# A new order for the first list of a fused attention, channel-mix and expert kernel, with one sigmoid tile moved to another ring

## The chip, the core and the metric

The kernel runs on one core of a Trainium2 chip. The metric is the device time of one execution in microseconds (us). Five engines work side by side, each in the order of its own instruction stream: TensorE (PE in the profile, with its weight loads as PEld), VectorE (DVE), ScalarE (ACT), GpSimd (POOL) and SyncE (SP, which issues most of the DMAs here).

## What is computed

Three layers follow one another. Attention inside chunks of 64 positions, a channel-mix layer, and four attention experts of which each token uses two. Cut to what matters:

```python
# 1: attention in chunks of 64
scores = scale * q_c @ k_c^T ; attn = softmax(scores) ; x = attn @ v_c        # B=8, H=8, S=576, D=64
# 2: channel mix, 512 -> 1024 -> 512
x_prev = x shifted by one position
xk = mu_k * x + (1 - mu_k) * x_prev ;  xr = mu_r * x + (1 - mu_r) * x_prev
k = relu(xk @ w_k) ;  v = (k * k) @ w_v ;  r = sigmoid(xr @ w_r)
x2 = r * v
# 3: four experts, two of them per token
for e in range(4): out += gate_e * (softmax(causal(x2 wq_e (x2 wk_e)^T)) @ (x2 wv_e) @ wo_e)
```

The change touches how layers 1 and 2 start. The channel-mix weights arrive as 64-bit floats and are turned into pairs of 32-bit numbers (high and low part) on the chip; every product of the mix is three TensorE products (high by high, high by low, low by high).

## The kernel before

Layers 1 and 2 work on 4608 tokens. A tile is 128 tokens (36 of them), a pair is two tiles, a unit is 384 tokens or three tiles (12 units). The order in which the first three units are worked on is written out by hand in the list `START` (L21): each word is a step, a letter with numbers, and `follow` (L492) calls the function of each step in turn. `in_line` (L482) ties each instruction to the one before it on the same engine, so every engine, SP with its DMA issues among them, runs its instructions exactly in the order of the list. Then `follow(TWO_UNITS, ...)` (L511) runs a second list four times for two units each, with unit numbers 2, 4, 6, 8 added and tile numbers 12, 18, 24, 30. The chain of `in_line` goes on from `START` into it.

The steps:

- `L`i, `A`i, `G`i, `B`i, `H`i, `O`i: one of 20 weight chunks of 128 x 512 (0 to 3 are w_r, 4 to 11 w_k, of which 8 to 11 hold columns 512 to 1023, 12 to 19 w_v). `L` issues its DMA of 512 KB on SP (L417), `A` is one ACT instruction (L423), `G` two DVE instructions (L427, L428), `B` one DVE (L432), `H` one POOL (L84), `O` one DVE (L443). Chunks 0 to 3 land in tiles of their own; chunks 4 to 19 share two staging tiles (`stb=2`), each free again after `B`.
- `lq`t, `lk`t, `lv`t: the loads of tile t of q, k and v on SP, two staging tiles each (`ldb=2`, `vb=2`). For t below 12 a tile is one to four DMAs (L158, L174). From t = 12 on, q and k are loaded by eight DMAs of 32 KB each (L151) and v by one or two (L166).
- `Tq`, `Tk`, `Eq`, `Ek`: the transposes of q and k on TensorE (L187) and their copies on ACT (L192); from t = 12 on `Tq` and `Tk` are one DVE transpose each (L197) and there is no `E` step. `S`j, `X`j, `U`j, `E`j, `Z`j, `Y`j: scores of pair j on TensorE and its softmax on DVE and ACT. `Tp`, `Ep`: the transposes of the result. `V`j: its product with v on TensorE (L270), the last reader of the two v tiles of pair j. `W`j: the result into `XT` (ACT, L82).
- `prev`u, then `a`, `b`, `c`, `d` with k or r, unit and block g: the mix with the shifted tokens (ACT L304, DVE L308, ACT L315, DVE L319).
- `r`u,m and `s`u,m: 12 TensorE products and the sigmoid (ACT, L344). `k`u,m, `K`u,m, `J`u,m: 12 products, three ACT instructions (L361 to L363), one DVE (L367). `v`u,m,h: 12 products, half h of w_v's rows. `y`, `z`, `x`, `D`: the product with the sigmoid (DVE L384), its split (POOL, DVE L393) and the store (POOL, L398).

The products of r, k and v go through three banks of PSUM (`mix`, `bufs=3`); a bank is free after `s`, the first instruction of `K`, or `y`. The sigmoids of a unit stand in one tile `sig`, of which there is one buffer, from the unit's first `s` to its last `y`. The ring `XT` has four buffers (`xb=4`), each for one unit's attention result.

The second list begins, with its tile numbers read as 13, 12 and so on and its unit numbers as 2 and 3 the first time:

```python
Tq1 Tq0 lq2 Tk1 k0,0 Tk0 prev1 ar1,3 ak1,0 k0,1 br1,3 K0,0 bk1,0 lk2 cr1,3 k0,2 J0,0 K0,1 ...
```

In the list before, the order on SP is `... L19 lk13 lq13 lv10 lv11 lv13 lv12`, with `lq12` and `lk12` earlier, and pair 5's `V5` stands between `v1,0,0` and `v1,0,1`.

Of the kernel before, what the change touches and what calls it, by code (L numbers as in the profile page):

```python
# [8 lines left out]
F32 = mybir.dt.float32  # L9
# [51 lines left out]
CFG = dict(ps=(2, 3, 1, 2), P=5, sm=3, load=5, lag=(3, 4), out=(5, 1), qk1=(1, 1), qk0=(9, 1.1), v=(10, 0.9), order=((3, 0), (2, 0), (0, 0), (4, 0), (1, 0), (3, 1), (2, 1), (0, 1), (1, 1)), after=1, conv='v', clo='v', chi='g', x2hi='g', x2lo='v', ylo='g', yhi='v', xt='aa', r2='av', klo='vv', amul='vv', nearly=2, x2b=1, yb=4, qb=4, direct=((0, 1), (1, 1), (1, 1)), tailAV=4, kp=2, yt=1, yf=2, zb=1, om=(3, 2, 1, 0, 4), hp=1000, x2d=2, early=(2, 1), dact=3, rate0=0.43, rate=0.45, sh=(10, 12, 2), sh2=(11, 1, -1), pro='cccqqaacavvcaaaaacaacaaaascc', alag=2, seq=0, end=2, outL=(11, 2), outE=2, kcp='aa', dsc='v', ldb=2, vb=2, cn=512, stb=2, xb=4, pa=5, tb=2, first_j=7, dve_j=6)  # L61
# [38 lines left out]
def attn_mix(tc, at, x2T, q, k, v, mu_k, mu_r, w_k, w_v, w_r, ident, attended_all, mixed_k):  # L100
# [5 lines left out]
    KD = DM // 128  # L106
# [8 lines left out]
    with ExitStack() as ctx:  # L115
        wts = ctx.enter_context(tc.tile_pool(name="wts", bufs=1))
        mx = ctx.enter_context(tc.tile_pool(name="mx", bufs=1))
# [5 lines left out]
        wkr = wkr_open.enter_context(tc.tile_pool(name="wkr", bufs=1, side="right"))  # L123
# [4 lines left out]
        mu = wkr.tile([128, 2, KD], F32, name="mu")  # L128
# [49 lines left out]
        qT, kT, PP, PT, XT = {}, {}, {}, {}, {}  # L178
# [147 lines left out]
        sig, kk = {}, {}  # L326
# [53 lines left out]
        X2 = {}  # L380
# [80 lines left out]
        def from_T(d, nm):  # L461
# [579 lines left out]
```

## Time and profile before

| | before |
|---|---|
| time, median of three runs | 991.43 us (989.77 to 992.68) |
| the profiled execution | 991.2 us, of which the span from first to last instruction is 987.9 us |
| busy over the span | PE 941.6 us (95%), DVE 668.1 (68%), ACT 625.8 (63%), POOL 190.8 (19%) |
| chain that ended last | PE 83% of the span, DVE 9%, DMA 4%, ACT 2% |
| mean granted TensorE clock | 0.991 of full speed |

The page cuts the span into 40 slices of 24.7 us; the digit of a slice is the busy share of an engine in tenths. Times in the rows below count from the start of the span. A row of a timeline says when an instruction began, how long it took, its engine, line and tiles, how many instructions are merged in it, and in brackets how long the engine was idle before it and which work ended the wait.

### The profile page before, as it was taken

What the parts mean: (1) busy time and instruction counts of PE and PEld (TensorE: products, weight loads), DVE (VectorE), ACT (ScalarE), POOL (GpSimd) and SP (SyncE); (2) the same over time, 40 slices, a digit from 0 to 9 for tenths busy, and PEclk for the clock granted to TensorE, in tenths of its full rate; (3) what the DMA queues carried; (4) which work ended last, traced back from release to release, by engine and by line L of the source; (5) the groups of instructions that cost most, each with busy time, mean ns of one, the idle gap of its engine ahead of it and who ended that gap; (6) DMA issues with size and microseconds to landing.
All of it is one profiled execution on the core that took longest, in us unless ns stands there. A gap on an engine that the chain in (4) does not pass through costs nothing.

```text
span 987.9 us, 21522 instructions
## 1 busy us (share of the span) xinstructions
PE 941.6 (95%) x8022; PEld 903.5 (91%) x8022; DVE 668.1 (68%) x1705; ACT 625.8 (63%) x1417; POOL 190.8 (19%) x336
## 2 busy tenths in 40 slices
PE   2688999999999999999999999999999999999997
PEld 1578999999999999999999999989989998999995
DVE  6988925655574657474746722687786787778895
ACT  3588663756756575667476823576675677567674
POOL 2111302011110102020202014323321323222101
PEclk9899999999999999999999999999999999999999
DMA  8977404343344335433513225565453645454312
GB/s 230 221 190 184 106 12 99 60 92 78 88 90 84 94 72 113 70 86 66 107 23 86 54 64 140 126 164 159 91 166 85 189 84 171 92 168 141 98 44 98
DMA packets 223408, 108.38 MB, mean 110 GB/s; under 512 B 187352, under 2 KB 199752, under 8 KB 223304
## 3 DMA queue, kind: packets, MB, share of 16 engines
q1 hardware_dynamic: 193032, 67.16, 30.0%
q0 software_dynamic: 30272, 39.86, 14.9%
q8 instruction: 63, 1.03, 0.4%
q14 instruction: 41, 0.34, 0.1%
HBM read 66.01 MB, written 28.38 MB: 96 GB/s over the span
## 4 chain that ended last, share of the span: by engine, by line
PE 83%; DVE 9%; DMA 4%; ACT 2%; issue 1%; SPq 0%; ACTq 0%; DVEq 0%
PE mps L95 16%; PE mps L97 16%; PE mps L96 16%; PE pj L95 6%; PE pj L96 6%; PE pj L97 6%; PE Sps L744 4%; PE Tps L804 3%; PE AVps L837 2%; DMA st<-in_moe_w_k_dram 2%; PE AVps L833 2%; PE Tps L187 2%; PE PVps L267 1%; PE Sps L211 1%; DVE PTl L811 1%
## 5 line engine op out<-in xcount | busy, mean ns | idle before, releaser
L95 PE MATMUL mps<-xhk,wkh 128*128 128x384 f32 x384 | 130.7, 340 | 0.8 <-POOL wkh L84 0.8
L367 DVE TENSOR_TENSOR kl<-r,kh 128x384 fp32r<-128x384 f32 x96 | 54.0, 563 | 114.5 <-ACT kh L363 114.5
L97 PE MATMUL mps<-xhk,wkl 128*128 128x384 f32 x384 | 129.1, 336 | 0.4 <-DVE wkl L443 0.4
L95 PE MATMUL mps<-kh,wvh 128*128 128x384 f32 x384 | 129.3, 338 | 0.0
L96 PE MATMUL mps<-xlk,wkh 128*128 128x384 f32 x384 | 129.0, 336 | 0.0
L96 PE MATMUL mps<-kl,wvh 128*128 128x384 f32 x384 | 128.4, 334 | 0.0
L97 PE MATMUL mps<-kh,wvl 128*128 128x384 f32 x384 | 128.4, 334 | 0.0
L756 ACT ACTIVATE P<-sm,nm 128x512 f32<-128x512 f32 (+3 forms) x144 | 83.8, 583 | 21.4 <-DVE nm L746 13.2
L84 POOL CAST x2d<-x2o 128x384 fp32r<-128x384 f32 x48 | 32.1, 671 | 322.2 <-DVE x2o L384 320.2
L746 DVE CUSTOM_DVE_ANT_0 sm<-Sps,mask 128x256 f32<-128x256 f32 (+4 forms) x160 | 74.7, 477 | 21.6 <-PE Sps L744 20.7
L811 DVE TENSOR_TENSOR PTl<-Tps,PTh 128x512 fp32r<-128x512 f32 (+2 forms) x144 | 70.2, 505 | 5.7 <-ACT PTh L810 4.1
L95 PEld LDWEIGHTS mps<-xhk,wkh 128*128 128x128 f32 x384 | 72.2, 188 | 1.5 <-POOL wkh L84 1.1
L97 PEld LDWEIGHTS mps<-xhk,wkl 128*128 128x128 f32 x384 | 72.2, 188 | 0.7 <-DVE wkl L443 0.7
L308 DVE SCALAR_TENSOR_TENSOR xa<-XT,mu,xa 128x384 f32<-128x384 f32 x96 | 57.7, 621 | 22.2 <-ACT xa L304 21.9
L95 PEld LDWEIGHTS mps<-kh,wvh 128*128 128x128 f32 x384 | 72.0, 188 | 0.7
L96 PEld LDWEIGHTS mps<-xlk,wkh 128*128 128x128 f32 x384 | 72.2, 188 | 0.0
L96 PEld LDWEIGHTS mps<-kl,wvh 128*128 128x128 f32 x384 | 72.1, 188 | 0.1
L97 PEld LDWEIGHTS mps<-kh,wvl 128*128 128x128 f32 x384 | 72.1, 188 | 0.0
L304 ACT ACTIVATE xa<-XT,mu 128x384 f32<-128x384 f32 x96 | 57.1, 616 | 19.5 <-DVE xlr L319 9.7
L810 ACT ACTIVATE PTh<-Tps 128x512 fp32r<-128x512 f32 (+2 forms) x144 | 61.7, 453 | 8.6 <-PE Tps L804 6.9
L95 PE MATMUL mps<-xhr,wrh 128*128 128x384 f32 x192 | 65.8, 343 | 0.0
L804 PE MATMUL Tps<-ident,P 128*128 128x128 f32 x384 | 63.6, 273 | 2.1 <-DVE PTl L811 0.8
(182 smaller groups left out, 2603.8 us busy)
## 6 DMA issues: line engine op xcount, KB each, us to landing
x2T<-x2d POOLq DMA_DIRECT2D x48, 384.0 KB, 3.0
x<-x2T POOLq DMA_DIRECT2D x32, 576.0 KB, 6.5
K<-Kph SPq DMA_DIRECT2D x64, 128.0 KB
out_dram<-o SPq DMA_DIRECT2D x32, 256.0 KB
ldq<-in_q_dram SPq DMA_DIRECT2D x192, 32.0 KB
ldk<-in_k_dram SPq DMA_DIRECT2D x192, 32.0 KB
ldv<-in_v_dram SPq DMA_DIRECT2D x21, 256.0 KB
st<-in_moe_w_k_dram SPq DMA_DIRECT2D x8, 512.0 KB
```

Source lines behind the costliest of these rows:

```text
L95: nc.tensor.matmul(out=out, lhsT=ah, rhs=bh, start=first and i == 0, stop=False)
L96: nc.tensor.matmul(out=out, lhsT=ah, rhs=bl, start=False, stop=False)
L97: nc.tensor.matmul(out=out, lhsT=al, rhs=bh, start=False, stop=last and i == n - 1)
L304: nc.scalar.activation(out=a, in_=XT[u][:, g, :, :SEG], func=ACTF.Copy, scale=mu1[:, w, g:g + 1])
L308: nc.vector.scalar_tensor_tensor(a, XT[u][:, g, :, 1:], mu[:, w, g:g + 1], a, op0=ALU.mult, op1=ALU.add)
L367: eng(nc, CFG["klo"][u >= CFG["nearly"]]).tensor_tensor(o.lo, K2.pop((u, m)), f32(o.hi), op=ALU.subtract)
L744: issued = nc.tensor.matmul(out=pp[:, :w], lhsT=x, rhs=y[:, a:a + w], start=n == 0, stop=n == len(terms) - 1)
L746: nc.vector.tensor_tensor_reduce(out=sm[:, a:a + w], in0=pp[:, :w], in1=mk[:, :w], op0=ALU.add, op1=ALU.min, scale=-scale, scalar=3e38, ac ...
L756: nc.scalar.activation(out=x[:, :nk], in_=sm[:, :nk], func=ACTF.Exp, scale=-1.0, bias=nm[:, :1], accum_out=z)
L804: nc.tensor.transpose(pp[:, j], x[:, j * 128:(j + 1) * 128], ident)
L810: nc.scalar.activation(out=h, in_=src, func=ACTF.Copy)
L811: nc.vector.tensor_tensor(l, src, f32(h), op=ALU.subtract)
```

## The change

The words of `START` are the same; their order is new. In the new list the four r steps of the second unit (`r1,0` to `r1,3`) and their sigmoids stand between the last k of the first unit and its first v, where the list before has them behind the last v of the first unit. So that the second unit's sigmoids can be written while the first unit's still stand in `sig`, `r_sig` takes for unit 1 a tile of the `XT` ring. `r_sig` makes the tile at the unit's first `s` step, whichever m it has, as the new list doesn't keep the order of m. On SP the new list's order of loads is

```text
L7 L3 L5 lk0 L6 lq0 L1 L14 lk1 lq1 L2 lk2 lk3 L4 lq2 lq3 lv1 L11 lv0 lq5 lq4 L0 lk5 lk4 L8 lv2 lv3 L19 lq7 lk6 lq6 lk7 lq8
lk8 lq9 lv5 lk9 lv4 lq11 L10 lk10 L9 lv7 lk11 lq10 L17 L18 lk13 lv6 L13 L12 L15 L16 lv9 lv8 lv11 lv10 lv13 lk12 lq13 lv12 lq12
```

The diff:

```diff
--- before.py
+++ after.py
@@ -19,26 +19,26 @@
 F64_BIAS = 2.0 ** -112
 
 START = """
-L3 L2 L1 L4 lq0 L5 lq1 A3 G3 lk0 lk1 B3 A2 G2 H3 O3 B2 A1 G1 H2 O2 G4 A4 Tq0 B1 Eq0 B4 H1 G5 L10 H4 O1 Tq1 O4 A5 Eq1
-Tk0 B5 H5 L13 Ek0 lv1 Tk1 O5 Ek1 A10 G10 S0 lk3 lq2 B10 lq3 A13 G13 H10 lk2 L0 mu X0 lv0 B13 Tk3 U0 H13 Ek3 Tq2 O13 E0
-O10 lq5 Tq3 Eq2 Z0 L7 lk5 Eq3 Tk2 Y0 Ek2 lk4 lq4 A0 G0 S1 L6 B0 Tp0 H0 X1 Tp1 Ep0 O0 Tq5 Ep1 U1 A7 V0 Eq5 G7 E1 Tk5 B7
-lv2 W0 Z1 H7 Tk4 Ek5 Ek4 Tq4 O7 L12 lv3 Y1 Eq4 A6 S2 G6 lk7 B6 lk6 Tp3 X2 H6 lq7 Tp2 lq6 Ep3 G12 A12 Ep2 U2 V1 B12 E2
-Tk7 O6 H12 lk9 W1 Z2 lv5 Tk6 Ek7 prev0 Ek6 O12 Tq7 ar0,3 Y2 lq9 ar0,0 lv4 Tq6 Eq7 br0,0 Tp4 Eq6 br0,3 Tp5 cr0,0 S3
-cr0,3 dr0,0 L15 Ep4 dr0,3 Tk9 lk8 ar0,1 X3 lq8 ar0,2 L8 Ek9 br0,2 Tq9 Ep5 br0,1 cr0,2 U3 cr0,1 V2 Eq9 dr0,1 E3 lv7
-dr0,2 G15 W2 r0,0 Z3 ak0,1 prev1 lv6 A15 r0,1 ak0,0 bk0,1 s0,0 Y3 Tq8 B15 ck0,1 r0,2 bk0,0 L11 H15 Eq8 dk0,1 lk10 s0,1
-O15 A8 G8 ck0,0 r0,3 s0,2 ak0,2 dk0,0 B8 ak0,3 A11 G11 Tk8 H8 L18 Tp6 s0,3 lq12 Tp7 Ek8 bk0,2 lk11 Tk10 Ep6 B11 S4
-ck0,2 bk0,3 L9 H11 Ep7 O8 ck0,3 V3 dk0,2 Ek10 dk0,3 A18 lv9 O11 k0,0 ar1,2 G18 W3 X4 ar1,0 k0,1 lv8 K0,0 B18 G9 H18 A9
-k0,2 L14 K0,1 U4 lq10 lk12 J0,0 E4 B9 k0,3 O18 H9 L17 J0,1 O9 K0,2 Tk11 Z4 k0,4 K0,3 G14 Tq10 A14 Y4 k0,5 Ek11 K0,4
-B14 J0,3 H14 L16 k0,6 A17 G17 lq11 Eq10 O14 K0,5 B17 Tp8 J0,2 H17 L19 k0,7 K0,6 J0,5 lk13 O17 G16 A16 v0,0,0 Ep8 J0,6
-K0,7 B16 G19 H16 A19 Tq11 Tp9 O16 Eq11 lq13 B19 Ep9 S5 J0,7 H19 J0,4 V4 O19 X5 v0,0,1 lv10 W4 br1,2 prev2 U5 cr1,2
-v0,1,0 lv11 br1,0 E5 dr1,2 y0,0 cr1,0 v0,1,1 ak1,2 Z5 z0,0 dr1,0 v0,2,0 bk1,2 ar1,3 x0,0 ck1,2 Y5 D0,0 v0,2,1 y0,1
-br1,3 z0,1 dk1,2 cr1,3 v0,3,0 x0,1 ar1,1 dr1,3 D0,1 y0,2 ak1,1 br1,1 z0,2 Tp11 bk1,1 cr1,1 v0,3,1 x0,2 Ep11 ck1,1
-dr1,1 D0,2 dk1,1 ak1,3 ak1,0 r1,0 bk1,3 y0,3 ck1,3 bk1,0 z0,3 dk1,3 ck1,0 r1,1 x0,3 ak2,1 dk1,0 s1,0 D0,3 bk2,1 r1,2
-ak2,3 s1,1 bk2,3 r1,3 s1,2 k1,0 s1,3 k1,1 K1,0 J1,0 k1,2 K1,1 J1,1 k1,3 K1,2 J1,2 k1,4 K1,3 J1,3 Tp10 K1,4 k1,5 Ep10
-J1,4 k1,6 K1,5 J1,5 k1,7 K1,6 J1,6 v1,0,0 K1,7 ck2,3 J1,7 V5 ck2,1 dk2,3 dk2,1 ak2,0 v1,0,1 lv13 ar2,0 bk2,0 W5 br2,0
-v1,1,0 cr2,0 y1,0 lv12 ck2,0 dr2,0 z1,0 dk2,0 ar2,1 x1,0 ak2,2 v1,1,1 br2,1 D1,0 bk2,2 cr2,1 ck2,2 dr2,1 v1,2,0 dk2,2
-ar2,2 y1,1 ar2,3 br2,2 z1,1 br2,3 cr2,2 v1,2,1 x1,1 cr2,3 dr2,3 D1,1 dr2,2 v1,3,0 y1,2 z1,2 x1,2 v1,3,1 D1,2 r2,0 y1,3
-z1,3 x1,3 r2,1 D1,3 s2,0 r2,2 s2,1 r2,3 s2,2 s2,3
+L7 A7 G7 B7 L3 G3 L5 H7 O7 A3 B3 H3 lk0 L6 lq0 Tq0 L1 A5 G5 B5 L14 H5 lk1 Tk0 O3 A6 G6 B6 lq1 Eq0 L2 Tk1 H6 O5 G1 O6
+A1 B1 A14 Ek1 G14 H1 O1 lk2 B14 H14 Ek0 G2 O14 Tq1 Eq1 S0 mu A2 B2 X0 H2 O2 lk3 L4 A4 Tk2 Ek2 U0 E0 G4 Z0 lq2 Tq2 lq3
+Eq2 Tk3 lv1 B4 Y0 Tq3 L11 G11 H4 Ek3 Eq3 S1 X1 A11 B11 H11 Tp1 Ep1 U1 lv0 Tp0 O11 Ep0 lq5 Tq5 lq4 V0 O4 E1 Z1 Y1 W0 L0
+Tq4 A0 lk5 G0 lk4 Tk5 L8 G8 Ek5 B0 Eq5 Eq4 H0 Tk4 Ek4 Tp3 Ep3 Tp2 Ep2 S2 X2 lv2 O0 lv3 L19 A8 V1 W1 prev0 U2 A19 G19
+ar0,2 br0,2 ar0,0 br0,0 E2 Z2 cr0,2 dr0,2 lq7 Tq7 lk6 Tk6 Eq7 cr0,0 dr0,0 Y2 lq6 Tq6 Eq6 lk7 Tk7 Ek6 ar0,1 br0,1 ar0,3
+Ek7 br0,3 cr0,1 lq8 Tq8 Tp4 B8 Ep4 lk8 S3 cr0,3 H8 Eq8 dr0,1 ak0,2 Tk8 Ek8 Tp5 lq9 Tq9 dr0,3 r0,0 r0,1 X3 bk0,2 lv5
+ak0,1 Ep5 bk0,1 Eq9 U3 O8 ck0,2 ck0,1 lk9 Tk9 B19 H19 lv4 V2 dk0,1 dk0,2 E3 Z3 lq11 Tq11 s0,1 r0,2 r0,3 Ek9 S4 ak0,0
+bk0,0 ak0,3 bk0,3 W2 prev1 ck0,3 ck0,0 L10 s0,3 G10 dk0,3 A10 s0,2 lk10 s0,0 dk0,0 k0,0 k0,1 k0,2 O19 L9 G9 B10 H10
+ar1,0 lv7 br1,0 A9 B9 lk11 Tk11 lq10 Tq10 H9 Eq11 O10 L17 Y3 K0,0 O9 K0,1 J0,1 L18 cr1,0 dr1,0 A17 ar1,1 lk13 K0,2 G17
+J0,0 ar1,2 A18 k0,3 Tp6 Ep6 br1,1 G18 k0,4 J0,2 lv6 k0,5 B18 H18 Tp7 cr1,1 K0,4 dr1,1 B17 O18 H17 J0,4 ar1,3 K0,3
+br1,2 cr1,2 br1,3 k0,6 k0,7 cr1,3 K0,6 L13 A13 L12 O17 J0,3 K0,7 dr1,2 dr1,3 r1,0 r1,1 G13 A12 Ep7 B13 H13 Eq10 s1,0
+L15 G12 B12 Ek11 V3 O13 J0,7 G15 s1,1 H12 O12 A15 W3 B15 L16 r1,2 Tk10 r1,3 A16 G16 Ek10 S5 s1,2 H15 O15 K0,5 B16 H16
+lv9 ak1,1 J0,6 J0,5 s1,3 v0,0,0 O16 v0,0,1 ak1,3 bk1,3 X4 v0,1,0 v0,1,1 ck1,3 v0,2,0 v0,2,1 bk1,1 ck1,1 dk1,1 U4 ak1,0
+E4 bk1,0 y0,1 z0,1 x0,1 D0,1 y0,0 dk1,3 ak1,2 bk1,2 ck1,0 dk1,0 v0,3,0 ck1,2 dk1,2 v0,3,1 k1,0 K1,0 z0,0 x0,0 y0,2
+z0,2 D0,0 k1,1 K1,1 Z4 Y4 Tp9 Tp8 Ep8 y0,3 lv8 X5 J1,1 U5 k1,2 k1,3 x0,2 Ep9 K1,2 k1,4 k1,5 J1,2 D0,2 J1,0 K1,3 J1,3
+K1,4 z0,3 x0,3 k1,6 k1,7 E5 J1,4 K1,5 K1,6 J1,5 K1,7 v1,0,0 J1,6 V4 W4 J1,7 v1,0,1 prev2 v1,1,0 ak2,1 D0,3 lv11 v1,1,1
+v1,2,0 v1,2,1 Z5 Y5 Tp10 bk2,1 y1,0 ar2,2 br2,2 v1,3,0 cr2,2 v1,3,1 z1,0 y1,1 x1,0 D1,0 dr2,2 ar2,0 br2,0 ck2,1 dk2,1
+cr2,0 dr2,0 ar2,3 br2,3 ar2,1 br2,1 Ep10 cr2,3 z1,1 x1,1 D1,1 Tp11 dr2,3 y1,2 z1,2 cr2,1 dr2,1 r2,0 r2,1 x1,2 ak2,3
+bk2,3 ck2,3 dk2,3 s2,0 ak2,2 y1,3 ak2,0 s2,1 r2,2 r2,3 z1,3 lv10 Ep11 V5 s2,2 x1,3 D1,3 bk2,0 ck2,0 s2,3 bk2,2 ck2,2
+lv13 lk12 D1,2 W5 lq13 lv12 lq12 dk2,0 dk2,2
 """.split()
 
 CH = 64
@@ -339,8 +339,11 @@
             mm3(nc, p, [((wr.hi[:, g, cc], wr.lo[:, g, cc]), rhs(XS[u, 1], g)) for g in range(KD)])
 
         def r_sig(u, m):
-            if m == 0:
-                sig[u] = mx.tile([128, KD, UNIT], F32, tag="sig", name="sig")
+            if u not in sig:
+                if u == 1:
+                    sig[u] = wkr.tile([128, KD, UNIT], F32, tag="XT", bufs=CFG["xb"], name="sig")
+                else:
+                    sig[u] = mx.tile([128, KD, UNIT], F32, tag="sig", name="sig")
             nc.scalar.activation(out=sig[u][:, m], in_=MB.pop(("r", u, m)), func=ACTF.Sigmoid)
 
         def mix_r(u, m):
```

## Rows read from the trace of the kernel before

**Rows 1.** The page: TensorE's share, and its busy tenths in 40 slices.

```profile
PE 941.6 (95%) x8022; PEld 903.5 (91%) x8022; DVE 668.1 (68%) x1705; ACT 625.8 (63%) x1417; POOL 190.8 (19%) x336
...
PE   2688999999999999999999999999999999999997
```

**Rows 2.** Windows of 10 us: busy time of each engine, granted clock, DMA share, GB/s.

```profile
core 0: us, PE busy (x) PEld busy (x) DVE busy (x) ACT busy (x) POOL busy (x), PEclk, DMA share, GB/s
0.00:10.00 10.00, 0.00 (x0) 0.00 (x0) 5.53 (x9) 3.32 (x4) 3.91 (x10) 1.00 0.81 240
...
40.00:50.00 10.00, 7.27 (x151) 5.80 (x149) 8.89 (x16) 6.04 (x13) 2.03 (x6) 0.77 0.95 208
...
90.00:100.00 10.00, 7.62 (x84) 7.25 (x87) 8.69 (x16) 8.74 (x18) 2.19 (x3) 1.00 0.68 171
```

**Rows 3.** Timeline of TensorE: `r0,0`, `v0,0,0`, `S4`, `V3`, `v0,0,1`, `k2,0`.

```profile
58.51 0.45 PE L95 MATMUL mps<-xhr,wrh 128*128 128x384 f32 x1
...
93.74 0.34 PE L95 MATMUL mps<-kh,wvh 128*128 128x384 f32 x1
95.83 0.60 PE L187 MATMUL Tps<-ident,ldq 128*128 128x128 f32 x4
...
99.86 0.69 PE L214 MATMUL Sps<-kT,qT 64*64 64x64 f32 x32 [2.38 <-ACT qT L192]
100.38 1.11 PE L270 MATMUL PVps<-PT,ldv 64*64 64x64 f32 x64
101.42 0.44 PE L95 MATMUL mps<-kh,wvh 128*128 128x384 f32 x1
...
168.36 0.34 PE L95 MATMUL mps<-xhk,wkh 128*128 128x384 f32 x1
```

**Rows 4.** Chain of waits, 60 to 102 us: `L9` (start, length, piece).

```profile
74.14 5.58 DMA st<-in_moe_w_k_dram
```

**Rows 5.** Timeline of VectorE: `G6`.

```profile
41.22 0.43 DVE L427 TENSOR_SCALAR st<-st 128x512 int32<-128x512 int32 x1 [0.84 <-DMA st<-in_moe_w_k_dram]
```

**Rows 6.** Timeline of SP: `lk12`'s eight DMAs, `lv13` with `lv12`, `lk17`'s eight.

```profile
82.24 4.45 SPq L151 DMA_DIRECT2D ldk<-in_k_dram  x8
...
145.02 1.95 SPq L166 DMA_DIRECT2D ldv<-in_v_dram  x3
...
175.71 4.02 SPq L151 DMA_DIRECT2D ldk<-in_k_dram  x8
```

**Rows 7.** Timeline of TensorE, then VectorE: `V5`; `Tq13` with `Tq12`, `Tk13` with `Tk12`.

```profile
144.27 1.16 PE L270 MATMUL PVps<-PT,ldv 64*64 64x64 f32 x64
...
161.88 1.30 DVE L197 STREAM_TRANSPOSE qT<-ldq 128x512 f32<-128x512 f32 x2
163.09 1.26 DVE L197 STREAM_TRANSPOSE kT<-ldk 128x512 f32<-128x512 f32 x2
```

**Rows 8.** Windows of 1 us, columns as in rows 2.

```profile
164.00:165.00 1.00, 1.00 (x8) 1.00 (x7) 0.36 (x1) 0.49 (x1) 0.00 (x0) 1.00 1.16 349
168.00:169.00 1.00, 1.00 (x7) 1.00 (x7) 0.00 (x0) 0.45 (x2) 0.00 (x0) 1.00 0.42 65
...
181.00:182.00 1.00, 1.00 (x7) 1.00 (x7) 0.15 (x1) 0.93 (x2) 0.00 (x0) 1.00 0.00 0
```

**Rows 9.** Timeline of ScalarE: `cr3,3`, then the first of `K2,1`.

```profile
172.14 0.51 ACT L315 ACTIVATE xhr<-xa 128x384 fp32r<-128x384 f32 x1
172.72 0.49 ACT L361 ACTIVATE r<-mps 128x384 f32<-128x384 f32 x1
```

**Rows 10.** Windows of 1 us, and a row of TensorE's timeline.

```profile
22.00:23.00 1.00, 0.00 (x0) 0.00 (x0) 0.85 (x2) 0.68 (x1) 0.00 (x0) 0.50 0.93 210
...
27.00:28.00 1.00, 1.00 (x7) 0.80 (x5) 1.00 (x2) 1.00 (x3) 0.00 (x0) 0.75 1.00 350
...
23.95 1.08 PE L187 MATMUL Tps<-ident,ldk 128*128 128x128 f32 x4 [5.45 <-DMA ldk<-in_k_dram]
```

**Rows 11.** Waits between 60 and 102 us: total, times, longest.

```profile
DVE st L427 <- DMA st<-in_moe_w_k_dram: 2.3, 2, 1.7
```

## The prediction

> **What bounds the kernel now.** I read the page first: TensorE is busy for 95% of the span, and its 40 slices say where it isn't, in the first four of 24.7 us; from then on every digit is 9 but the last [rows 1]. So the first list can be worth only what TensorE loses before 100 us, and whatever it loses after that goes into the time undiminished. The windows then show how: 0 of the first 10 us busy, 7.27 from 40 to 50, 7.62 from 90 to 100, with the DMA engines 81% to 95% busy early and VectorE 87% to 89% busy in both later windows [rows 2].
>
> To compare the two lists I use one measure, **lateness**: the time at which a TensorE step begins, less the TensorE work that stands ahead of it in the list. That work is counted with 2.09 us for each r, k or half v step, 1.04 for a V or S [rows 3] and about 0.4 for four transposes, 117 us for the whole list in either order. In the list before, `r0,0` begins at 58.5 with 16.4 us ahead of it: 42.1 late. `v0,0,0` has 46.3 ahead and is 47.4 late, `v0,0,1` has 51.2 ahead and is 50.2 late. The first product behind the list, `k2,0`, begins at 168.36, so 51 late [rows 3]; nothing is lost in between. So of the list's 51 us, 42 are gone before the first mix product, and 8 more while the weights of v come in: `V3` and `S4` wait, and `v0,0,1` needs chunk 19, the last of 16 that pass through two staging tiles. `L9` on the chain takes 5.58 us to land [rows 4], and its tile can be loaded again only when it has been joined.
>
> **The early part of the new list: about 0.7 us gained.** Until 42 us the DMA engines set the pace. `G6` of before waited for its landing until 41.22 [rows 5], with 10 weight chunks and 14 tiles of q, k, v issued up to it. In the new order the last of that kind is `G8`, with 11 chunks and 14 tiles. A chunk is 0.52 MB at 240 GB/s, so 2.2 us; a tile 0.26 MB at 208, so 1.25 [rows 2]. `G8` comes at 43.3. `r0,0` stands behind `Tq9`, whose load is 1 chunk and 9 tiles further on: 43.3 + 2.2 + 11.3 = 56.8, with the copy 57.2. Its work ahead is 15.8, so it is 41.4 late instead of 42.1.
>
> **r of the second unit ahead of v: 7.5 us gained.** With `k0,0` to `k0,7` and four r steps, 8.4 us of TensorE work now stand where the weights of v used to be awaited. The late chunks follow one another through the staging tiles. At 41.4 late and with 26.8 ahead, `k0,0` begins at 68.2, and `Tk11`, behind three k steps, is done at 74.9. `L13` stands on SP behind `lk13`, eight DMAs for which `Tk11` must be done, and `lv6`, four more [rows 6]: 74.9 + 4.4 + 2.6 = 81.9. With 5.5 us to a landing [rows 4] it is there at 87.4; `G13` and `B13` take 1.6, so `L15` goes at 89.0 and lands at 94.5, and `L16`, behind `B12`, at 96.1. `A16` stands ahead of `Ek10` on ScalarE, so `S5` begins at 97.4 rather than at 96.3 and `v0,0,0` at 98.4. The weights of `v0,0,1` are ready at 100.7, when TensorE gets there. Lateness at `v0,0,0`: 98.4 - 55.6 = 42.8. By then all 20 chunks are converted, and what VectorE still has to do in the list is less than TensorE has. I take 43.0. The list then ends at 117.1 + 43.0 = 160.1, against 168.36: **8.2 us earlier**. Both ends: nothing lost behind `r0,0` gives 158.5, a gain of 9.9; each of the four last round trips of the staging tiles late by 1.3 us, about a quarter of a landing, gives 165.3, a gain of 3.
>
> **The sigmoid tile: nothing.** It is the same 128 sigmoid writes; its ring buffer is free again after the last `y` of unit 1. The ring's next takers, units 4 and 5 in the second list, come behind that. Exponentials and sigmoids change places as often in both lists, so the table loads on ScalarE stay the same in number.
>
> **The end of the new list: 12.7 us lost.** `V5`, in the old list at 144.27 [rows 7], is now the last TensorE step. `lv13` needs a v tile that only `V5` frees, for there are two and both hold tiles 10 and 11. SP works in the list's order, so `lk12`, `lq13`, `lv12` and `lq12`, which need nothing from `V5`, stand queued behind that wait. And the second list begins on VectorE with the transposes of exactly tiles 13 and 12. Before, they ran at 161.88 to 164.35, loaded long since [rows 7].
>
> From the end of `V5`, called T: `lv13` is two DMAs of 0.65 [rows 6], 1.3. Three loads of eight DMAs are 4.02 to 4.45 each [rows 6], 12.6, and `lv12` 0.65: T + 14.5. The row of `lk17` ends at 179.73, and no byte moved from 181 on [rows 8]: the landing is 1.3 later, T + 15.8. `Tq12`, `Tk13`, `Tk12` at 0.62 each [rows 7]: T + 17.7. Behind them on VectorE comes `br3,3`, and on ScalarE `cr3,3`, which waits for it and stands ahead of `K2,1` (in the old trace at 172.14 and 172.72 [rows 9]). At 0.5 each: T + 18.7. The first ACT of `K2,1`, 0.49 [rows 9], frees its bank at T + 19.2. TensorE has three banks and gets one back from `K2,0`, which stands ahead of `cr3,3`, so it does `k2,0` to `k2,3`, 8.3 us, and stands still for **10.9 us**. With the rows' shortest and longest loads it is 10.4 to 11.7.
>
> The clock adds to that. After TensorE had stood for 5.45 us up to 23.95, its granted clock was 0.50 of full speed, the 1.2 GHz level, and it was on its way back in the microsecond from 27 [rows 10]. That is 3.8 us at half speed, so 1.9 lost; I take 1.8, with 0 (no fall) and 2.7 as ends.
>
> **Sum.** The profiled execution took 991.2 us, 3.3 more than its span; its time is within 0.3 us of the median of three. 991.2 - 8.2 + 10.9 + 1.8 = **995.7 us**. The ends give 991.2 - 9.9 + 10.4 = 991.7 and 991.2 - 3 + 14.4 = 1002.6.
>
> **Rivals.** *The end of the list binds nothing* (faster, 983.0): the loads behind `lv13` get in before they are needed. The point is 8.3 us behind `V5`, when TensorE has used its banks; for that the three loads would have to move as the DMA queue does at its best, 349 GB/s in the microsecond from 164 [rows 8], 0.79 MB in 2.3 us instead of 12.6. Then `K2,1` frees its bank at T + 8.9, and all but 0.6 us of the wait is gone. Against it: while SP issued these loads in the old trace, the queue moved 65 GB/s at 0.42 of its engines' share [rows 8], so issuing sets their pace, not moving. The Trainium skill, in "DMA: Bandwidth & Descriptors", section "Issuing engines are not separate DMA queues", calls the sequencer's time to start a DMA usually small relative to the DMA itself; by that rule this rival would hold, and the rows disagree, 0.5 us for each 32 KB.
>
> *Evens out* (990 to 994): the early gain is at its upper end, 9.9, the loads at their lower, and the clock doesn't fall: 991.7. The digit and windows allow each of the three singly.
>
> *The early gain doesn't come* (1000 to 1004): `L13` to `L16` slip, since each waits for a join that waits for the landing before it, and SP has eight small DMAs ahead of `L13`. For it speaks that VectorE waited 2.3 us, in two places, for such landings between 60 and 102 us in the old trace [rows 11]; against it that TensorE has 8.4 us more work to cover them.
>
> **Chances.** Forecast (994.5 to 1000) 0.50; evens out 0.28; early gain doesn't come 0.13; end binds nothing 0.09. What a measurement of this kernel can tell from no change is about 0.3%, 3 us. Faster by more than that 0.09, within it 0.28, slower 0.63. The range reaches over the evens case and most of the third: 990 to 1002.
>
> **What would show it.** In the new profile: `r0,0` near 57 us; `v0,0,0` near 98; TensorE without a gap from there to about 160; then a gap of about 11 us some 8 us behind `V5`, with SP issuing eight DMAs three times in a row just before it, VectorE idle until `ldq` lands, and a window or two at half clock behind it. If the gap is missing, the forecast is wrong by its largest term; if `k2,0` comes later than 165, the early part is.

## The result: 1000.2 us, 0.95% slower than before

The changed kernel takes 1000.22 us (median of four, 999.93 to 1000.86). The kernel before, run beside it, took 990.6 (989.76 to 992.68); the ratio is 1.0095, with a 95% interval of 1.0076 to 1.0113. The profiled execution took 1000.0 us, of which 998.0 are its span (991.2 and 987.9 before).

Behind `r_sig` the lines of the changed kernel stand three higher than before: the sigmoid is L347, the first instruction of `K` L364. First the page, TensorE's busy tenths and its granted clock in 40 slices:

```profile
PE 946.5 (95%) x8022; PEld 908.4 (91%) x8022; DVE 670.2 (67%) x1705; ACT 624.0 (63%) x1417; POOL 192.2 (19%) x336
...
PE   2699998699999999999999999999999999999997
...
PEclk9699999799999999999999999999999999999999
```

Against [rows 1] the early slices are fuller, but an 8 and a 6 have come in at 150 to 200 us, and the clock has a dip in the second of these two slices. The timeline of TensorE shows three steps of the list, `r0,0`, `v0,0,0` and `k2,0`, and then `k2,4`:

```profile
57.65 0.42 PE L95 MATMUL mps<-xhr,wrh 128*128 128x384 f32 x1
...
99.16 0.45 PE L95 MATMUL mps<-kh,wvh 128*128 128x384 f32 x1
...
161.63 1.16 PE L270 MATMUL PVps<-PT,ldv 64*64 64x64 f32 x64
162.72 0.44 PE L95 MATMUL mps<-xhk,wkh 128*128 128x384 f32 x1
...
182.56 0.69 PE L95 MATMUL mps<-xhk,wkh 128*128 128x384 f32 x1 [11.26 <-ACT r L364]
```

`r0,0` begins at 57.65 (58.51 before), `k2,0` right behind `V5` at 162.72 (168.36 before, [rows 3]). So the list ends 5.64 us earlier. Then TensorE stands for 11.26 us. SP's queue and VectorE's timeline of the changed kernel show why:

```profile
162.38 1.27 SPq L166 DMA_DIRECT2D ldv<-in_v_dram  x2
163.71 5.00 SPq L151 DMA_DIRECT2D ldk<-in_k_dram  x8
168.75 3.90 SPq L151 DMA_DIRECT2D ldq<-in_q_dram  x8
172.75 0.40 SPq L166 DMA_DIRECT2D ldv<-in_v_dram  x1
173.19 7.98 SPq L151 DMA_DIRECT2D ldq<-in_q_dram  x16
```

```profile
174.65 0.71 DVE L197 STREAM_TRANSPOSE qT<-ldq 128x512 f32<-128x512 f32 x1 [11.42 <-DMA ldq<-in_q_dram]
179.18 0.71 DVE L197 STREAM_TRANSPOSE qT<-ldq 128x512 f32<-128x512 f32 x1 [3.82 <-DMA ldq<-in_q_dram]
179.81 1.26 DVE L197 STREAM_TRANSPOSE kT<-ldk 128x512 f32<-128x512 f32 x2
181.00 1.11 DVE L308 SCALAR_TENSOR_TENSOR xa<-XT,mu,xa 128x384 f32<-128x384 f32 x2
```

The five loads go out one after another from the moment `V5` runs: `lv13`, `lk12`, `lq13`, `lv12`, and `lq12` as the first half of the 16. VectorE waits 11.42 us for the first `ldq`, then 3.82 for the second; before, the same transposes began at 161.88 [rows 7]. ScalarE's `cr3,3` ends that chain (181.61, idle 14.90 us before it, for VectorE's `xa`), and `K2,1` behind it frees the bank.

Counted at the same TensorE instruction, the changed kernel is 5.64 us ahead at `k2,0` and 8.21 behind 80 products later, so the end of the list costs 13.85. Of that 11.4 is the stall, counted from the start of `k2,3` to that of `k2,4`, and 2.3 the clock: the 32 products from `k2,4` on took 7.87 us, where they take 5.55 before. The last 0.1 lies between `k2,0` and `k2,3`. The other 1.9 of the spans' difference of 10.1 come later (below).

### The profile page after: what moved, and what is told of

The parts are those of the page before. It is cut to its first block, busy times and chain, and to the rows that moved or that the text cites. A ratio compares the mean times of both kernels' runs of the same rounds, so it can differ in the third digit from the quotient of the medians.

```text
span 998.0 us, 21524 instructions
## 1 busy us (share of the span) xinstructions
PE 946.5 (95%) x8022; PEld 908.4 (91%) x8022; DVE 670.2 (67%) x1705; ACT 624.0 (63%) x1417; POOL 192.2 (19%) x336
## 4 chain that ended last, share of the span: by engine, by line
PE 84%; DVE 8%; DMA 3%; SPq 1%; ACT 1%; issue 1%; POOL 0%; ACTq 0%; POOLq 0%; DVEq 0%
PE mps L95 17%; PE mps L97 16%; PE mps L96 16%; PE pj L95 6%; PE pj L96 6%; PE pj L97 6%; PE Sps L747 4%; PE Tps L807 3%; PE AVps L840 2%; PE Tps L187 2%; PE AVps L836 2%; DMA st<-in_moe_w_k_dram 2%; PE PVps L267 1%; PE Sps L211 1%; DVE PTl L814 1%
## 5 line engine op out<-in xcount | busy, mean ns | idle before, releaser
L364 ACT ACTIVATE r<-mps 128x384 f32<-128x384 f32 x96 | 46.6, 485 | 34.5 <-PE mps L97 34.1
```

The costliest lines, as they stand in the source:

```text
L364: nc.scalar.activation(out=r, in_=MB.pop(("k", u, m)), func=ACTF.Relu)
```

## The experiments

One table for all runs, from the same rows of each trace. "Stall" is the idle time ahead of `k2,4` (in the run with a load from ScalarE, ahead of `k2,3`); "clock" is what the products from there on took beyond 5.55 us for 32. Times are medians, or one execution for those without a ratio, which show the stall in their trace rather than the time; in us.

| kernel | `r0,0` | `k2,0` | stall | clock | time | ratio to before (95%) |
|---|---|---|---|---|---|---|
| before | 58.51 | 168.36 | none | none | 990.6 | |
| changed | 57.65 | 162.72 | 11.26 | 2.3 | 1000.2 | 1.0095 (1.0076 to 1.0113) |
| three loads early | 59.76 | 164.85 | none | none | 987.2 | 0.9944 (0.9930 to 0.9959) |
| one load early | 58.50 | 163.65 | 7.43 | 2.7 | 996.5 | |
| `V5` early | 56.66 | 162.17 | 2.82 | 0.1 | 988.6 | |
| old list, new end | 59.40 | 167.59 | 11.02 | 2.7 | 1003.8 | 1.0114 (1.0093 to 1.0134) |
| sigmoid tile alone | 60.01 | 170.98 | none | none | 993.1 | 1.0007 (0.9997 to 1.0016) |
| `y0,2` ahead of `K1,0` | 58.32 | 162.47 | none | none | 985.8 | 0.9936 (0.9920 to 0.9951) |
| one load from ScalarE | 57.54 | 162.61 | 5.43 | 2.1 | 992.4 | |
| split DMAs | 59.01 | 164.59 | 14.85 | 1.8 | 1004.5 | |
| `r1` behind `v0` | 57.38 | 170.72 | none | none | 994.6 | 1.0029 (1.0018 to 1.0039) |

The kernel before ran beside each of the nine lower kernels too and gave medians of 991.5 to 992.6 there, so a time compares with that of the changed kernel only to some 2 us, and through the ratio where there is one.

### Three loads ahead of the wait

```diff
-... z1,3 lv10 Ep11 V5 ... ck2,2 lv13 lk12 D1,2 W5 lq13 lv12 lq12 dk2,0 dk2,2
+... z1,3 lv10 lk12 lq13 lq12 Ep11 V5 ... ck2,2 lv13 D1,2 W5 lv12 dk2,0 dk2,2
```

> The new list with one edit: lk12, lq13 and lq12 are issued right behind lv10, so ahead of lv13 and of its wait for V5; V5 stays the last TensorE step. My theory (the 24 DMAs stand on SP behind the wait of lv13) says that k2,0 begins at 162.7 us as in the changed kernel, that TensorE goes on behind k2,3 without the 11.3 us stall and at full clock, and that the time is 1000.2 - 11.3 - 2.1 = 986.8 us. Rival (VectorE or ScalarE are themselves late at the end of the list, the loads only seem to be): the stall stays, 1000 us. Second rival (the stall goes, but what it gave is lost again later, in the second list): 988 to 996 us with no stall at 171 us.

987.2 us, 13.0 less than the changed kernel: 0.56% under before instead of 0.95% over it. `k2,0` came at 164.85 instead of 162.7, as far behind as `r0,0` was (59.76 against 57.65). VectorE's timeline of this kernel, at the same place as above:

```profile
164.80 0.56 DVE L319 TENSOR_TENSOR xlk<-xa,xhk 128x384 fp32r<-128x384 f32 x1 [1.52 <-ACT xhk L315]
165.28 1.30 DVE L197 STREAM_TRANSPOSE qT<-ldq 128x512 f32<-128x512 f32 x2
166.50 1.26 DVE L197 STREAM_TRANSPOSE kT<-ldk 128x512 f32<-128x512 f32 x2
```

All four transposes follow one another without a wait, and `k2,4` follows `k2,3` (173.27, no idle time). The loss was the order of SP's queue, nothing of the computation. Neither rival holds: the stall is gone, and its gain stays to the end.

### One load ahead of the wait

```diff
-... z1,3 lv10 Ep11 V5 ... lv13 lk12 D1,2 W5 lq13 lv12 lq12
+... z1,3 lv10 lk12 Ep11 V5 ... lv13 D1,2 W5 lq13 lv12 lq12
```

> The new list with only lk12 moved ahead of lv13 (behind lv10); lq13, lv12 and lq12 stay behind the wait. My theory (SP's issue of eight DMAs per load sets the pace) says the stall shrinks by that load's time on SP, 5.0 us in the changed kernel's trace, to 6.3 us: 995.2 us if the clock falls as before, 993.1 if it doesn't. Rival (the queue moves the bytes at its best rate and a load is worth 0.75 us): stall 10.5 us, 999.5 us. Rival (only the last landing counts, however much stands ahead of it): stall 11.3 us, 1000.2 us.

The stall is 7.43 us, 3.8 shorter, not 5.0. In the changed kernel `lk12` took 5.00 us because one of its eight DMAs took 1.38 us on SP, where the ones beside it took 0.45:

```profile
166.83 0.45 SPq L151 DMA_DIRECT2D ldk<-in_k_dram  x1
167.33 1.38 SPq L151 DMA_DIRECT2D ldk<-in_k_dram  x1
```

Each of the nine kernels that load these tiles at or near the list's end has one such DMA among them, of 1.1 to 1.6 us. Here it was one of `lq13`'s, so that `lq13` took 5.11 us and `lq12` 4.03; with three loads early or `V5` early it was one of `lq12`'s. What makes it long, no row shows. It stays when a load goes early, so what a load less saves is about 3.9. Both rivals (0.75 us, nothing) are far off.

### `V5` earlier

```diff
-... Tp11 dr2,3 y1,2 z1,2 cr2,1 dr2,1 r2,0 r2,1 ... z1,3 lv10 Ep11 V5 s2,2
+... Tp11 dr2,3 y1,2 z1,2 cr2,1 dr2,1 Ep11 lv10 V5 r2,0 r2,1 ... z1,3 s2,2
```

> The new list with Ep11, lv10 and V5 moved to just ahead of r2,0, four r steps or 8.5 us earlier; the loads stay in their order behind lv13. My theory (all counts from the end of V5) says that lv13 goes out at about 153.9 instead of 162.4, the stall is 11.3 - 8.5 = 2.8 us, and the clock doesn't fall or falls for less: 989.6 us without a fall, 991.7 with all of it. Rival (V5 is not what the loads wait for): stall as it is, 1000.2 us.

2.82 us of stall against 2.8 expected, 988.6 us against 989.6, and `lv13` at 153.06. In the windows of 170 to 176 us TensorE stands for that time and its granted clock stays at 1.00:

```profile
170.00:172.00 2.00, 1.29 (x8) 0.97 (x6) 1.28 (x3) 0.00 (x0) 0.00 (x0) 1.00 0.44 68
172.00:174.00 2.00, 0.00 (x0) 0.00 (x0) 2.00 (x5) 0.84 (x2) 0.00 (x0) 1.00 0.42 65
174.00:176.00 2.00, 1.89 (x11) 1.89 (x12) 1.38 (x4) 1.94 (x5) 0.00 (x0) 1.00 0.43 66
```

(The columns are the window, its length, busy time of PE, PEld, DVE, ACT and POOL with their instructions, the granted clock, the DMA share and GB/s.) So either end of the wait can be moved.

### The old list with the new end

```diff
-... J1,7 V5 ck2,1 dk2,3 dk2,1 ak2,0 v1,0,1 lv13 ar2,0 bk2,0 W5 ... y1,0 lv12 ... r2,3 s2,2 s2,3
+... J1,7 ck2,1 dk2,3 dk2,1 ak2,0 v1,0,1 ar2,0 bk2,0 ... y1,0 ... r2,3 s2,2 V5 s2,3 lv13 lk12 W5 lq13 lv12 lq12
```

(`lq12`, `lk12` and `lq13` leave their earlier places too.)

> The kernel before with the end of the new list: V5 behind r2,3, and behind it lv13, lk12, lq13, lv12, lq12 in that order; all else of the old list stays. My theory (the loss is the end's, whatever stands ahead of it) says that k2,0 begins at 168.4 to 169.4 us (V5 ahead of it in either case), that a stall of about 11 us follows k2,3 with a fall of the clock worth 2 us, and that the time is 990.6 + 13.4 = 1004 us. Rival (the end costs only because the new list comes there 5.6 us earlier with VectorE's work undone): 991 to 997 us.

1003.8 us, a stall of 11.02 and 2.7 lost to the clock; `k2,0` came at 167.59, 0.8 ahead of the expected range. From `k2,0` to 80 products later the end costs 14.0 us here and 13.9 in the changed kernel, though the old list comes there 4.9 us later. So the end costs the same behind either list: the middle of the list gains, its end loses.

### The sigmoid tile alone

```diff
 def r_sig(u, m):
-    if m == 0:
-        sig[u] = mx.tile([128, KD, UNIT], F32, tag="sig", name="sig")
+    if u not in sig:
+        if u == 1:
+            sig[u] = wkr.tile([128, KD, UNIT], F32, tag="XT", bufs=CFG["xb"], name="sig")
+        else:
+            sig[u] = mx.tile([128, KD, UNIT], F32, tag="sig", name="sig")
```

> The old list with the new r_sig: only the tile of unit 1's sigmoids comes from the XT ring, the order of all work stays. My theory says nothing changes up to the end of the first list (k2,0 at 168 us, apart from the scatter of the early loads, which was 1.5 us either way in the runs so far), and the time is that of before within 0.3%: 989 to 993 us. The runs with the new list needed 265.8 us from the 80th product of the second list to the last units of the loop where those with the old list needed 265.5; if the ring's changed turn of tiles is the cause, this run shows 265.8 too. Rival (the ring's missing tile holds up units 4 and 5): several us more in that stretch and 994 us or more in all.

Ratio 1.0007 (0.9997 to 1.0016): nothing. `k2,0` came at 170.98, later than the scatter that was allowed for. Of the 2.6 us against before, 1.5 are `r0,0`'s and 1.0 are the clock's: `S4` waited 2.37 us, as it did before [rows 3], but here the clock fell to half behind it and came back between 105 and 106.

```profile
101.12 0.69 PE L214 MATMUL Sps<-kT,qT 64*64 64x64 f32 x32 [2.37 <-ACT qT L192]
...
104.00:105.00 1.00, 1.00 (x5) 1.00 (x4) 1.00 (x3) 0.36 (x2) 0.00 (x0) 0.50 0.29 55
```

The stretch that I had asked about took 265.53 us, as with the old list, so the 0.26 us more that the new lists take there are not the ring's doing; what they are stays open.

### `y0,2` ahead of `K1,0`

Every new list so far lost 0.8 us at `k1,1`. In the changed kernel:

```profile
118.83 0.44 PE L95 MATMUL mps<-xhk,wkh 128*128 128x384 f32 x1 [0.64 <-ACT r L364]
```

It waits for `K1,0`, though VectorE's timeline has `y0,2` at 113.51 for 0.56 us, which freed a bank 4 us earlier. My reason: steps get their banks in the order of the list, and there `K1,0` stands ahead of `y0,2`. The edit goes on top of the three loads:

```diff
-... v0,3,1 k1,0 K1,0 z0,0 x0,0 y0,2 z0,2 D0,0 k1,1
+... v0,3,1 k1,0 z0,0 x0,0 y0,2 K1,0 z0,2 D0,0 k1,1
```

> The kernel with lk12, lq13, lq12 behind lv10, and one more edit: K1,0 is written behind y0,2 instead of ahead of z0,0, so that k1,1 gets the bank that y0,2 has freed and not the one that K1,0 frees last. My theory for the 0.8 us that every new list has lost at k1,1 says that this loss goes: the lateness at k1,2 is at most 0.2 us above that at k1,0 (0.9 until now), and the time is 987.2 - 0.7 = 986.5 us. Rival (the wait only moves on to k1,2 or k1,3, since K1,0 now comes later on ScalarE): lateness at k1,4 0.9 us above that at k1,0 as before, 987.2 us.

Lateness, with 0.39 us for four transposes, is 43.56 at `k1,0` and 43.56 at `k1,2`: the wait is gone. The time, 985.8 us, is the lowest of all, 0.64% under before (0.49% to 0.80%). Its 1.4 us against the run with the loads alone are within the spread of the two (984.3 to 988.9 and 986.1 to 988.0); the 0.8 of the trace are what is shown.

### One load from ScalarE

```diff
-nc.sync.dma_start(out=x[r:r + 32, :, w],
+(nc.scalar if (nm, t) == ("q", 12) else nc.sync).dma_start(out=x[r:r + 32, :, w],
```

> The new list unchanged, but the eight DMAs of lq12 are issued by ScalarE instead of SP, at their place in the list. My theory (the issuing engine's time for each DMA sets the pace, not what moves) says that lq12 goes out beside lk12 on SP and VectorE finds it there: the last load that it waits for is lq13, 3.9 us earlier than lq12 was, the stall is 11.4 - 3.9 = 7.5 us and the time 996.3 us. Rival (the loads share one limit whoever issues them): lk12 and lq12 slow each other, the stall stays at 11.4 us and the time at 1000.2 us.

The two queues of this kernel:

```profile
163.60 4.07 SPq L151 DMA_DIRECT2D ldk<-in_k_dram  x8
167.71 4.94 SPq L151 DMA_DIRECT2D ldq<-in_q_dram  x8
...
166.65 6.23 ACTq L151 DMA_DIRECT2D ldq<-in_q_dram  x8
```

All 24 DMAs are out at 172.9 instead of 177.2 in the changed kernel, and VectorE's second wait is gone. ScalarE, busy with its DMAs until 172.9, came late with `K2,0`, so TensorE already stood ahead of `k2,3`, for 5.43 us. (Why it began them only at 166.65, 2.8 us after its last work, no row shows.) `k2,4` began at 178.59, 4.0 us earlier than in the changed kernel and 7.7 late against before, close to the 7.5 expected. But the clock fell in the wait ahead of `k2,3`, so the 2.0 us that it cost were spent on `k2,3`, inside those 7.7, and not on top of them: that is why 996.3 was too high. For the question asked it is enough: the loads don't share one limit that would have kept the stall at 11.4. ScalarE's eight went out one in 0.78 us, SP's one in 0.49 to 0.64, so some of it may be shared.

### Split DMAs

```diff
+for e in range(2 if (nm, t) == ("k", 12) else 1):
+    h = slice(e * H // 2, (e + 1) * H // 2) if (nm, t) == ("k", 12) else slice(0, H)
-    nc.sync.dma_start(out=x[r:r + 32, :, w], in_=src[b, :, ...])
+    nc.sync.dma_start(out=x[r:r + 32, h, w], in_=src[b, h, ...])
```

> The new list unchanged, but lk12 is issued as 16 DMAs of half the heads each instead of eight, with the same bytes in the same pieces of 128 bytes. If each DMA costs SP its 0.5 us whatever it holds, lk12 takes 9 to 10 us on SP instead of 5.0, the stall grows by 4 to 5 us and the time is 1004 to 1005 us. Rival (the pieces or the bytes set the pace): lk12 takes 5 us as before, stall 11.4 us, 1000.2 us.

The load on SP, and the windows while it goes out and while the whole-size ones behind it do:

```profile
165.58 8.88 SPq L153 DMA_DIRECT2D ldk<-in_k_dram  x16
174.51 3.89 SPq L153 DMA_DIRECT2D ldq<-in_q_dram  x8
```

```profile
168.00:172.00 4.00, 4.00 (x25) 4.00 (x25) 0.00 (x0) 0.55 (x2) 0.00 (x0) 1.00 0.18 29
172.00:176.00 4.00, 1.18 (x7) 0.86 (x5) 0.00 (x0) 0.00 (x0) 0.00 (x0) 1.00 0.25 37
176.00:178.00 2.00, 0.00 (x0) 0.00 (x0) 0.00 (x0) 0.00 (x0) 0.00 (x0) 1.00 0.42 65
```

The same bytes in 16 DMAs take 8.88 us instead of 5.00, and the queue moves 29 GB/s instead of 65. The stall grows by 3.6. One of the 16 is the long one again, of 1.57 us; another is

```profile
171.65 0.43 SPq L153 DMA_DIRECT2D ldk<-in_k_dram  x1
```

So 16 KB take 0.43 us where 32 KB took 0.45: SP pays for each DMA, nearly whether it holds 16 or 32 KB.

### `r1` behind `v0`

The last kernel with `r1,0` to `r1,3` and `s1,0` to `s1,3` taken from between `K0,7` and `v0,0,0` and put behind `v0,3,1`:

```diff
-... K0,7 dr1,2 dr1,3 r1,0 r1,1 ... r1,2 Tk10 r1,3 ... S5 s1,2 ... s1,3 v0,0,0 ... v0,3,1 k1,0
+... K0,7 dr1,2 dr1,3 ... Tk10 ... S5 ... v0,0,0 ... v0,3,1 r1,0 s1,0 r1,1 s1,1 z0,0 x0,0 y0,2 r1,2 s1,2 r1,3 s1,3 k1,0
```

> The kernel of the run before with y0,2 ahead of K1,0 and the loads early (985.8 us), with one part of the change taken back: the four products r1,0 to r1,3 and their sigmoids stand behind v0,3,1 instead of ahead of v0,0,0; loads, joins and all else stay where they are. My theory (these 8.4 us of TensorE work cover the wait for the last weights of v) says that v0,0,0 is reached 8.4 us earlier, at about 91.5 us, but its weights come at 97.8 as before and those of v0,0,1 at 100.4: the lateness at k1,0 is 6.4 to 6.9 us more than the 43.6 it was, and the time 992 to 993 us (994 to 995 if the clock falls in the wait). Rival (the new list brings the weights early enough in any case, and the gain over the old list comes from the order of loads and joins): lateness at k1,0 44 to 45 us, 986 to 987 us.

Lateness at `k1,0` is 51.82, 8.26 more, and the time 994.6: the order of the loads and joins alone gains nothing, the four r steps are what covers the wait. The wait isn't at `v0,0,0` itself. TensorE stands at `V3` for 3.14 us and at `S5` for 1.98, each time for a copy on ScalarE (L192), and `v0,0,0` follows at 98.85. `S5`'s copy stands on ScalarE behind the scaling of a late weight chunk, which waited for its landing:

```profile
91.46 2.46 PE L270 MATMUL PVps<-PT,ldv 64*64 64x64 f32 x64 [3.14 <-ACT PT L192]
...
96.94 1.98 PE L214 MATMUL Sps<-kT,qT 64*64 64x64 f32 x64 [1.98 <-ACT kT L192]
...
95.71 0.69 ACT L426 ACTIVATE cz<-st 128x512 f32<-128x512 f32 x1 [0.51 <-DMA st<-in_moe_w_v_dram]
96.31 0.58 ACT L192 ACTIVATE kT<-Tps 128x512 f32<-128x512 f32 x1
```

`V3`'s copy, at 90.82, stands there behind the work of `K0,7` and the scaling of a chunk that did not wait for its landing, so it came late mostly by ScalarE's own work. The clock falls to half while TensorE stands at `V3`, and `S5` and `v0,0,0` take 5.0 us together, where they take 3.3 in the changed kernel; that is more than the 1.4 beyond the 6.9 expected:

```profile
90.00:92.00 2.00, 0.53 (x8) 0.35 (x8) 1.86 (x4) 2.00 (x5) 0.74 (x1) 0.65 0.44 115
...
94.00:96.00 2.00, 0.96 (x4) 0.55 (x4) 1.97 (x5) 1.50 (x5) 0.00 (x0) 0.50 0.77 248
...
98.00:100.00 2.00, 2.00 (x40) 1.88 (x33) 2.00 (x4) 1.39 (x3) 0.88 (x1) 0.50 0.44 98
```

## The prediction, point by point

The forecast was 995.7 us within 990 to 1002, slower at 0.63. It is slower, by the mechanism that was forecast for the end of the list; the time is 4.5 us above the forecast, just outside the band of 994.5 to 1000 that had 0.50, at the lower edge of the rival that let the early gain fail.

**The early part: about right, but not to be told from one trace.** `r0,0` came 0.86 us earlier; 1.3 were forecast (57.2). The same early steps gave 56.66 to 59.76 in the eight kernels with the new list and 58.51 to 60.01 in the three with the old. The means, 58.1 and 59.3, differ as forecast; a single trace of the new list can be 1.7 off its mean. The path to it was another, so the close number is in part luck. The forecast bound `r0,0` to the landing of `Tq9`'s load, but in the changed kernel's trace the last landing that TensorE waited for is that of `Tk6`; from there on it had no idle time, and its clock was at half from 51 to 54 (the last row is a window, as in [rows 2]):

```profile
50.78 0.99 PE L187 MATMUL Tps<-ident,ldk 128*128 128x128 f32 x4 [1.30 <-DMA ldk<-in_k_dram]
...
57.24 0.66 PE L187 MATMUL Tps<-ident,ldq 128*128 128x128 f32 x4
...
52.00:54.00 2.00, 2.00 (x11) 1.76 (x10) 1.99 (x3) 1.20 (x3) 0.00 (x0) 0.50 0.72 164
```

**r of the second unit ahead of v: right in kind, too large.** `v0,0,0` came at 99.16 (98.4 forecast), TensorE has no gap over 0.25 us between 51 and 118, and the last chunk of w_v was converted at 99.85 (99.17 and 0.68), 1.5 us before `v0,0,1` at 101.38. The run with `r1` put back shows the cause. But `k2,0` came at 162.72 instead of 160.1. From `r0,0` on, 102.9 us were forecast and 105.07 measured. Two terms were wrong. The list's work was put at 117 us; at the prediction's own prices 44 steps of 2.09, 12 of 1.04 and 36 of 0.4 make 118.8, and the measured starts fit 118.5. The old list's end was a measured time, so the missing 1.5 made only the new one look early. And nothing was to be lost behind `v0,0,0`, but `k1,1` lost 0.8. The sum of gains was 5.6, not 8.2.

**The sigmoid tile: right**, by the run of it alone. (The "128 sigmoid writes" are 48 instructions in the trace, in either kernel.)

**The end of the list: right, step by step.** `V5` ends at 162.79, which is T. `lq12` left SP at T + 14.4 (14.5 forecast), `Tq12` began at T + 16.4 (15.8), the transposes were done at T + 18.3 (17.7), and `K2,1`'s first instruction was done at T + 19.7 (19.2). The landing was 2.0 us rather than 1.3; the rest fits, where two misses offset each other: `lv13` began 0.4 us ahead of T and was out at T + 0.9 (1.3), and `lk12` took 5.00 us, longer than the longest load of the range. Stall 11.26 against 10.9. What the runs add: it goes with SP's order (three loads early), by 3.8 us per load (one early), with `V5` (moved early), and comes with both into the old list.

**The clock: 2.3 instead of 1.8**, within the ends given (0 to 2.7). In the four other kernels that stood for 5.43 us or longer it cost 1.8 to 2.7. The windows of the changed kernel:

```profile
172.00:173.00 1.00, 0.00 (x0) 0.00 (x0) 0.00 (x0) 0.00 (x0) 0.00 (x0) 1.00 0.47 73
174.00:175.00 1.00, 0.00 (x0) 0.00 (x0) 0.35 (x1) 0.00 (x0) 0.00 (x0) 0.50 0.94 211
...
186.00:187.00 1.00, 1.00 (x5) 1.00 (x4) 0.67 (x2) 0.94 (x4) 0.00 (x0) 0.50 0.48 73
187.00:188.00 1.00, 1.00 (x6) 1.00 (x5) 0.45 (x1) 1.00 (x3) 0.00 (x0) 0.78 0.37 58
188.00:189.00 1.00, 1.00 (x7) 1.00 (x7) 0.68 (x2) 0.94 (x4) 0.00 (x0) 1.00 0.47 72
```

The engine had stood since 171.3; the 1.2 GHz level shows from 174 on. It worked again from 182.56, and 2.4 GHz came back between 187 and 188. [rows 10] had shown the same fall on a shorter stall.

**What was not foreseen: 1.9 us behind the list.** 0.35 us of it come up between 190 and 552 us in every kernel with the new list and in none with the old. 1.1 us fall between 911 and 929 in this execution and don't show in six of the seven others with the new list, so they belong to the execution. The last 0.4 us fall at 868 us, in this execution and in four of the seven others. Why, no run shows. The time around the span was 2.0 us instead of 3.3.

So the 4.3 us between 995.7 and the profiled 1000.0 are, to 0.1: 2.6 of early gain that was counted too high, 0.5 of stall (11.4 between the starts), 0.5 of clock, 1.9 behind the list, less 1.3 around the span.

**The rivals.** *The end binds nothing* fell: a load is worth 3.8 us, not its 0.75 us of moving. Where the end was mended and did bind nothing, the time was 985.8 instead of its 983.0, with `k2,0` at 162.47 instead of 160.1. The Trainium skill, in "DMA: Bandwidth & Descriptors", section "Issuing engines are not separate DMA queues", says that starting DMAs on several engines saves only the sequencer's time, which it calls usually small. That the loads share the engines may be seen in ScalarE's 0.78 us per DMA; that the time to start one is small doesn't hold here, with 0.45 us for 32 KB, whose moving would take 0.09 at the 349 GB/s of [rows 8], and 0.43 for 16 KB. *The early gain doesn't come* holds in part: 5.6 of 8.2 came, and by another cause than it named, since `L13` to `L16` did not slip far enough to delay `v0,0,1`.

## What to carry to other kernels

In a list that fixes the order of every engine, a load that must wait for a buffer holds back every load behind it: put those that need nothing ahead of it, or free the buffer earlier; here the first turned 0.95% lost into 0.56% gained. Count a load by its DMAs on the issuing engine where they are small, since there that, not the bytes, is its time. When two orders are compared, use the same count of work for both sides, measured or summed, and see how far the same steps scatter from run to run before a gain of one microsecond is claimed.

## What the runs showed of the hardware

A DMA of 16 KB took SP 0.43 us and one of 32 KB 0.45, but for one in each run that took 1.1 to 1.6; halving the size about halved the rate of the queue, from 65 to 29 GB/s. Issued from ScalarE beside SP, eight DMAs of 32 KB took 6.23 us, and ScalarE did nothing else in that time. TensorE's granted clock stayed at 1.00 after a stand of 2.82 us (`V5` early) and of 2.38 (before, at `S4`). It fell to 0.50 behind one of 2.37 (sigmoid tile alone, at `S4`) and within one of 3.14 (`r1` behind `v0`, at `V3`), and was at 0.50 after 5.43 us and more. So the length of a stand alone didn't decide whether the clock fell; what else did, no run here shows.
